# Whole float32 weights for the first unit of an attention and MoE kernel, split into two parts after that use

## The chip, the cores and the metric

The kernel runs on one core of a Trainium2 chip. The time is that of one execution on the device, in microseconds (us). The core has five engines with a queue of their own each: TensorE (PE in the profile; its weight loads are PEld), VectorE (DVE), ScalarE (ACT), GpSimd (POOL) and SyncE (SP), which issues the transfers here. An instruction waits at the head of its engine's queue until what it needs is there, so the order in which each queue is filled is part of the kernel.

## The reference

Attention over 4 batches, 8 heads, 768 positions and a head size of 64. Each position sees a window of 15 positions to either side and one summary key and value for each block of 32 positions (the maximum of the keys, the mean of the values). The result goes, as 3072 rows of 512, through two matrix products with a pointwise function between them:

```python
scores_l = scale * np.matmul(q, k.transpose(0, 1, 3, 2))          # window only
scores_s = scale * np.einsum('bhsd,bhnd->bhsn', q, k_sum) + np.log(block)
a = softmax(concatenate([scores_l_m, scores_s]))
x = matmul(a, concatenate([v, v_sum]))       # (3072, 512) after a transpose
h = x @ w_in                                 # w_in is (512, 2048)
g = h - np.tanh(h)
return (g @ w_out).astype(np.float32)        # w_out is (2048, 512)
```

The two weights are given as 64-bit floats, the result is float32.

## The kernel before

**Units.** The rows are cut into 8 units (NU) of 384 (U), two to a batch. The MoE of a unit runs over 16 blocks f of the hidden dimension (NF). For each, `moe_in` (L884) makes a 128x384 block of h in PSUM from four chunks of x, `moe_act_small` (L896) and what follows it make g from it, and `moe_out` (L944) adds g times a 128x512 block of w_out to three result tiles of 128x512, y. After f = 15 `store_y` copies the tiles out of PSUM and stores them. Attention of the later units runs beside it: in the loop over slots at the end (L1017), the MoE lags by 22 slots (LAG), 16 of which make a unit.

**Precision.** A product of two float32 operands that are held as they are is called whole here. From two operands split into a high and a low part of type float32r, a product is made as high by high, low by high and high by low, three instructions to a whole product's one call. In the kernel before, `moe_in` is split for every unit; `moe_out` is whole for unit 0 and f in WHOLE_F = {0 ... 6}, and split otherwise. `x_split` (L873) makes the two parts of x out of PSUM, `moe_split` (L938) those of g.

**Weights.** `convert(i)` (L468) brings block i of 32 (even: w_in, odd: w_out) in: a transfer of 512 KB of 64-bit words into one of three buffers (`wraw`), then the bit work that makes float32 of it in a buffer `tmp` (two) or `qa` (one): "w scale" on ScalarE or VectorE, "w shift" and "w low" on VectorE, the sign on VectorE ("w sign"), or on ScalarE and GpSimd ("w sign 1", "w sign 2") for the blocks in SIGNED. Then "w high part" (ScalarE or VectorE) and "w low part" (GpSimd or VectorE) write the two halves of the tile `w`. For the seven whole blocks the sign step writes the float32 tile `wf` instead, and `split_whole` (L528), called right after unit 0's `moe_out` of the block, makes `wh` from it, the difference in `tmp`, and a copy of that ("w low part 3") into the memory of `wf`.

**Order.** Nothing is issued in the order of the code. `do` and `either` record a task with its engines and their prices; `Plan.schedule` (L155) simulates the engines at build time, takes for each the ready task with the longest path behind it, and so fixes one order for all queues. A task with several engines gets its first one unless that is busy by more than a slack. Nudges to the path lengths and slacks are held in tables by the kind and count of a task (BIAS, KB, SL) and by thirds of the run (HALF, by count). `ring` gives a tile the memory of an earlier one of the same tag, and has it wait for all tasks that touched that one. Until 100 us (WARM) idle time of TensorE is filled with small products (`keep_warm`).

The program stands twice in the kernel; the second stands under a condition on the largest sum of squares (L283) and isn't run with these inputs.

Of the kernel before, what the change touches and what calls it, by code (L numbers as in the profile page):

```python
# [28 lines left out]

WHOLE_F = {0, 1, 2, 3, 4, 5, 6}  # L30

# [40 lines left out]
class Task:  # L72
    __slots__ = ("index", "costs", "go", "after", "order", "level", "count", "ready", "next", "start", "engine", "cost", "place", "out", "banks", "behind", "moves", "kind", "name")


# [22 lines left out]
class Plan:  # L98
# [56 lines left out]
    def schedule(self, idle):  # L155
# [16 lines left out]
        free = dict.fromkeys(engines, 0.65)  # L172
        dma = 0.0
        clock = Clock()
# [30 lines left out]
        while total:  # L205
# [20 lines left out]
            if e == PE and idle is not None:  # L226
                cost, go = idle
                if now > free[PE]:
                    free[PE] = max(free[PE], min(now, getattr(tasks[0], "out", now) + self.SEEN[POOL]))
                while free[PE] < WARM and now - free[PE] > 2 * cost + 0.1:  # L230
                    d = Task()
                    d.after, d.order, d.behind = tasks[:1], (), ()
                    d.start, d.engine, d.go = free[PE], PE, go
                    d.out = free[PE] = clock.run(free[PE], cost)
                    done.append(d)
                now = max(now, free[PE])
            t.start, t.engine, t.cost = now, e, t.costs[e]
            t.behind = [at - self.SEEN[a] for b in t.banks for a, at in used.get(b, {}).items() if a != e]
# [49 lines left out]
def program(  # L288
# [101 lines left out]
    def dma(kind, go, nbytes, run, r=(), w=()):  # L390
        do(kind, SP, nbytes / 360e3 * (2 if run < 512 else 1), go, r, w)


    fixed(("ident",), [P, P])
    fixed(("mask",), [P, SC])
    fixed(("blk",), [P, 3, NBH])
# [10 lines left out]
    def make_mask():  # L407
        gpsimd.memset(mask, 0.0)

        for lo, hi, off in ((0, 64, 0), (64 + NB, SC, 64)):  # L410
            m = mask[:, lo:hi]
            gpsimd.affine_select(m, m, [[1, hi - lo]], ALU.is_ge, BIG, base=off, channel_multiplier=-1)
            gpsimd.affine_select(m, m, [[-1, hi - lo]], ALU.is_ge, BIG, base=2 * WIN - off, channel_multiplier=1)
        gpsimd.memset(mask[:, 64:64 + NB], -LOG32)

# [13 lines left out]

    for f in range(NF):  # L430
        fixed(("w", 2 * f), [P, 2, DM], F32R)
        if f in WHOLE_F:

            buf(("wf", f), f"wf{f}", [P, DM])
            fixed(("wh", f), [P, DM], F32R)
        else:
            fixed(("w", 2 * f + 1), [P, 2, DM], F32R)

    for j in range(2):
        buf(("qf", j), f"q{j}", [P, U])  # L440
        buf(("kf", j), f"k{j}", [P, 2, KC])
    fixed(("rawq",), [P, NT, HG, D])
    fixed(("rawk",), [P, 4, HG, D])
# [24 lines left out]
    def convert(i):  # L468
# [4 lines left out]
        def load():  # L473
# [3 lines left out]
            else:  # L477
                sync.dma_start(at(raw), w_out[f * P:(f + 1) * P, :].bitcast(U32))
        dma("w load", load, P * 8 * DM, 1024, w=[(raw, 0), (raw, 1)])
        buf(tmp, "tmp", [P, DM], F32, 2) if i % 3 else buf(tmp, "qa", [P, DM], F32, 1)  # L480
# [17 lines left out]

        whole = i % 2 == 1 and f in WHOLE_F
        to = (("wf", f), 0) if whole else (tmp, 0)  # L500

# [37 lines left out]
    def top_bases(b, g):  # L539
# [3 lines left out]
        return ("th", b, g), ("tl", b, g)  # L543

    def mean_base(b, g):
        return buf(("mean", b, g), f"mean{g}", [P, HG * D], F32, 1)

# [65 lines left out]
    def place_v(b, g, tag):  # L613

        ps, x, mean = bank(("mv", b, g), tag), ("sum", b, g), mean_base(b, g)
# [5 lines left out]
        do("mean out", ACT, 0.28, lambda: scalar.activation(at(mean)[:NB], at(ps)[:NB, :HG * D], AF.Copy), r=[(ps, 0)], w=[(mean, 0)])  # L621
# [43 lines left out]
    def finish_v(b, g):  # L665
        acc, ps, mean = ("acc", 1, b, g), bank(("mv", b, g), "pT"), mean_base(b, g)
# [5 lines left out]
        do("mean out", ACT, 0.28, lambda: scalar.activation(at(mean)[:NB], at(ps)[:NB, :HG * D], AF.Copy, scale=1.0 / 32), r=[(ps, 0)], w=[(mean, 0)])  # L672

# [42 lines left out]
    def put_mean(u, g):  # L716

        mean = ("mean", u // 2, g)
        for half in range(2):
            r = 64 * (1 - half)  # L720
            dma("mean put", lambda r=r, half=half: sync.dma_start(vw[r:r + NB, :, half].rearrange("r i h d -> r i (h d)"), at(mean)[:NB].unsqueeze(1).broadcast_to([NB, NT, HG * D])),
                NT * NB * HG * D * 4, 1024, r=[(mean, 0)], w=[vw_keys(i, half)[2] for i in range(NT)])

# [82 lines left out]
    def softmax(u, p, i):  # L806
# [3 lines left out]
        def first(a):  # L810
# [6 lines left out]
            for half in range(2):  # L817
                rows, cs = slice(64 * half, 64 * half + 64), slice(64 * half, 64 * half + N2)
                vector.tensor_tensor_reduce(at(pr)[rows, a], o[rows, cs], mask[rows, cs], 1.0, 3e38, ALU.add, ALU.min, at(st)[rows, a:a + 1])

# [63 lines left out]
    def moe_in(u, f):  # L884
        xh, xl, w, ph = ("xh", u), ("xl", u), ("w", 2 * f), bank(("ph", u, f), "pH")

        def go():
            w4 = at(w).rearrange("p a (c n) -> p a c n", c=NC)
            o = at(ph)[:, :U]
            for c in range(NC):  # L890
                tensor.matmul(o, w4[:, 0, c], at(xh)[:, c], start=c == 0, stop=False)
                tensor.matmul(o, w4[:, 1, c], at(xh)[:, c], start=False, stop=False)
                tensor.matmul(o, w4[:, 0, c], at(xl)[:, c], start=False, stop=c == NC - 1)
        do("in", PE, 1.956, go, r=[(w, 0), (w, 1)] + [(x, c) for x in (xh, xl) for c in range(NC)], w=[(ph, 0)])

# [48 lines left out]
    def moe_out(u, f):  # L944
        g, w = g_base(u, f), ("w", 2 * f + 1)
        whole = u == 0 and f in WHOLE_F
        if whole:
            keys = [(g, 0), (("wf", f), 0)]
        elif f in WHOLE_F:
            keys = [(("gh", u, f), 0), (("gl", u, f), 0), (("wh", f), 0), (("wl", f), 0)]  # L950
        else:
            keys = [(("gh", u, f), 0), (("gl", u, f), 0), (w, 0), (w, 1)]
        for i in range(NT):
# [4 lines left out]
            def go(i=i, y=y):  # L958
                s = slice(P * i, P * (i + 1))
                if whole:  # L960
                    tensor.matmul(at(y), at(g)[:, s], at(("wf", f)), start=f == 0, stop=f == NF - 1)
                    return
                gh, gl = at(("gh", u, f))[:, s], at(("gl", u, f))[:, s]
                high, low = (at(("wh", f)), at(("wl", f))) if f in WHOLE_F else (at(w)[:, 0], at(w)[:, 1])
# [175 lines left out]
```

## Time and profile before

| | |
|---|---|
| time, median of three runs | 792.17 us (789.04 to 793.16) |
| the profiled execution | 788.95 us |
| its span, first to last instruction | 787.2 us |
| mean granted TensorE clock | 0.973 of full speed |
| TensorE busy, share of the span | 92% |
| VectorE busy | 67% |
| ScalarE busy | 55% |
| GpSimd busy | 37% |
| moved by DMA | 61.05 MB, mean 78 GB/s |

The profile is of one execution. A row of a group gives the line, the engine, the operation, the tile written and the tiles read, the shape, how often it ran, then the busy time in us and the mean duration in ns, then the idle time of the engine just before these instructions and what ended it. All instructions carry line 69, a helper that issues them in the planned order, so groups are told apart by their tiles: `pH` is the PSUM tile of moe_in, `pY` that of moe_out, `pS`, `pT` and `pX` those of attention. Where the memory of one tile is taken by another, a row can show an older name: the low part of a whole weight shows as `wf`. A view by stretches gives, for each stretch of the span, the time that each engine was busy (and its instructions), the granted clock, and what the DMA engines did.

### The profile page before, as it was taken

Reading aid. Unit: us, or ns where it says so; the run is one execution under the profiler, and the core shown is the slowest. Engines: PE = TensorE matmul, PEld = TensorE weight load, DVE = VectorE, ACT = ScalarE, POOL = GpSimd, SP = SyncE. Lnnn points to the kernel's source line nnn. Section 1 sums busy time; section 2 is a strip of 40 time slices with the busy share of each in tenths; the row PEclk is TensorE's granted clock in tenths of the full one; section 3 lists DMA queues with packets and bytes.
Section 4 is the critical chain, followed back from the end, with each engine's and each line's share of the span. In section 5 each row is a group of like instructions: output and inputs, shape, how many; then the busy total and the mean of one; then the engine's idle time right before and its main releaser. Section 6 shows DMA issues by size and latency. Waiting matters only on the chain.

```text
span 787.2 us, 13950 instructions
## 1 busy us (share of the span) xinstructions
PE 725.2 (92%) x4464; PEld 615.8 (78%) x4464; DVE 527.7 (67%) x1776; ACT 437.0 (56%) x1286; POOL 290.0 (37%) x390
## 2 busy tenths in 40 slices
PE   8888887777989999989899999999999999999995
PEld 6567554666878888868788888888888898889994
DVE  4878999999766767496676667476567657662221
ACT  3557765456546656546465557556665556654232
POOL 3023556666533233546323323522333232432221
PEclk9869999989999999999999999999999999999998
DMA  9876484433411121050411121031303021101001
GB/s 231 235 195 176 136 203 141 132 103 91 128 32 37 42 77 44 20 138 26 134 42 38 42 78 42 20 69 47 74 1 79 1 79 42 38 2 41 1 0 46
DMA packets 121523, 61.05 MB, mean 78 GB/s; under 512 B 92512, under 2 KB 113248, under 8 KB 121440
## 3 DMA queue, kind: packets, MB, share of 16 engines
q1 hardware_dynamic: 121440, 60.06, 28.2%
q8 instruction: 38, 0.62, 0.3%
q14 instruction: 45, 0.37, 0.2%
HBM read 51.38 MB, written 6.29 MB: 73 GB/s over the span
## 4 chain that ended last, share of the span: by engine, by line
PE 65%; DVE 23%; DMA 3%; issue 3%; ACT 2%; POOL 2%; SPq 0%; POOLq 0%; DVEq 0%; ACTq 0%
PE pH L69 27%; PE pY L69 26%; DVE prob L69 6%; PE pS L69 6%; DVE tmp L69 4%; PE pT L69 4%; DVE qa L69 3%; DVE top L69 2%; PE pX L69 2%; DVE k L69 2%; DVE stat L69 1%; POOL wraw L69 1%; DVE gl L69 1%; DMA wraw<-in_moe_w_out_dram 1%; DVE w L69 1%
## 5 line engine op out<-in xcount | busy, mean ns | idle before, releaser
L69 PE MATMUL pH<-xh,w 128*128 128x384 f32 x1024 | 273.5, 347 | 15.3 <-POOL w L69 7.9
L69 POOL TENSOR_TENSOR gv<-gu,gt 128x384 f32<-128x384 f32 x116 | 118.3, 1020 | 315.4 <-ACT gu L69 184.2
L69 PEld LDWEIGHTS pH<-xh,w 128*128 128x128 f32 x1024 | 187.9, 192 | 29.3 <-POOL w L69 11.2
L69 PE MATMUL pH<-xl,w 128*128 128x384 f32 x512 | 175.3, 342 | 1.0 <-DVE xl L69 1.0
L69 ACT ACTIVATE gu<-pH 128x384 f32<-128x384 f32 x128 | 62.5, 488 | 172.5 <-PE pH L69 164.2
L69 PE MATMUL pY<-w,gh 128*128 128x512 f32 x432 | 140.7, 407 | 0.0
L69 DVE CUSTOM_DVE_ANT_0 prob<-pS,mask 64x118 f32<-64x118 f32 x352 | 97.9, 278 | 42.6 <-PE pT L69 28.5
L69 ACT ACTIVATE prob<-prob,stat 128x118 f32<-128x118 f32 x195 | 76.4, 393 | 58.1 <-DVE stat L69 52.2
L69 PEld LDWEIGHTS pH<-xl,w 128*128 128x128 f32 x512 | 98.3, 192 | 1.7 <-DVE xl L69 1.7
L69 DVE CAST gh<-gv 128x384 fp32r<-128x384 f32 x74 | 30.4, 410 | 85.7 <-POOL gv L69 79.2
L69 PE MATMUL pY<-w,gl 128*128 128x512 f32 x216 | 85.1, 394 | 0.7 <-DVE gl L69 0.7
L69 PEld LDWEIGHTS pY<-w,gh 128*128 128x128 f32 x432 | 75.0, 190 | 10.9 <-issue 0.5
L69 PE MATMUL pY<-wf,gh 128*128 128x512 f32 x189 | 79.2, 442 | 0.0
L69 ACT ACTIVATE gu<-gu 128x384 f32<-128x384 f32 x128 | 66.7, 522 | 0.0
L69 PE MATMUL pS<-k,q 128*128 128x364 f32 (+1 forms) x176 | 48.9, 357 | 14.7 <-DVE stat L69 12.1
L69 ACT ACTIVATE gt<-pH 128x384 f32<-128x384 f32 x128 | 61.7, 482 | 0.1
L69 PE MATMUL pY<-wh,gh 128*128 128x512 f32 x147 | 61.5, 418 | 0.0
L69 DVE TENSOR_TENSOR gl<-gv,gh 128x384 fp32r<-128x384 f32 x90 | 54.1, 601 | 7.4 <-ACT gh L69 2.3
L69 PE MATMUL pY<-wh,gl 128*128 128x512 f32 x147 | 58.4, 397 | 0.0
L69 DVE TENSOR_SCALAR prob<-prob,stat 128x118 f32<-128x118 f32 x184 | 55.3, 337 | 2.3
L69 PEld LDWEIGHTS pS<-k,q 128*128 128x128 f32 x176 | 29.4, 192 | 30.4 <-issue 18.8
L69 DVE TENSOR_SCALAR stat<-stat 128x2 f32<-128x2 f32 x95 | 27.9, 294 | 31.3 <-ACT prob L69 31.0
(161 smaller groups left out, 1164.3 us busy)
## 6 DMA issues: line engine op xcount, KB each, us to landing
wraw<-in_moe_w_in_dram SPq DMA_DIRECT2D x16, 512.0 KB
wraw<-in_moe_w_out_dram SPq DMA_DIRECT2D x16, 512.0 KB
rawq<-in_q_dram SPq DMA_DIRECT2D x48, 128.0 KB
out_dram<-tmp SPq DMA_DIRECT2D x24, 256.0 KB
rawk<-in_k_dram SPq DMA_DIRECT2D x32, 128.0 KB
vw<-in_v_dram SPq DMA_DIRECT2D x40, 96.0 KB
vw<-in_v_dram SPq DMA_DIRECT2D x48, 64.0 KB
wraw<-in_k_dram SPq DMA_DIRECT2D x16, 192.0 KB
```

Source lines behind the costliest of these rows:

```text
L69: return lambda *args, **kwargs: self._tc.keep_in_program_order(op(*args, **kwargs))
```

## The change

All 32 weight blocks are whole for unit 0, and so is x of unit 0: `x_split` makes one float32 copy in the memory of the high part, `moe_in` of unit 0 multiplies whole, `moe_out` of unit 0 is whole for all f, and g of unit 0 is not split. `split_whole` is called after each of these uses. It writes the high part to a tile of its own and the low part straight into the float32 tile of the block before it in the order of use (into a tile `wl` for the first), which "w low part 3" is dropped for. The units from 1 on use the two parts as before.

```diff
-WHOLE_F = {0, 1, 2, 3, 4, 5, 6}
+WHOLE_IN = True
+WHOLE_F = set(range(16))
...
+    wholes = sorted((i for i in range(2 * NF) if (WHOLE_IN if i % 2 == 0 else i // 2 in WHOLE_F)), key=lambda i: i // 2 + 1.5 * (i % 2))
+    for i in range(2 * NF):
+        if i in wholes:
+            buf(("wf", i), f"wf{wholes.index(i)}", [P, DM])
+            fixed(("wh", i), [P, DM], F32R)
         else:
-            fixed(("w", 2 * f + 1), [P, 2, DM], F32R)
+            fixed(("w", i), [P, 2, DM], F32R)
...
-        whole = i % 2 == 1 and f in WHOLE_F
-        to = (("wf", f), 0) if whole else (tmp, 0)
+        whole = i in wholes
+        to = (("wf", i), 0) if whole else (tmp, 0)
...
-    def split_whole(f):
+    def split_whole(i):
 
-        x, high, tmp, low = ("wf", f), ("wh", f), buf(("wd", f), "tmp", [P, DM], F32, 2), buf(("wl", f), f"wf{f}", [P, DM], F32R)
+        n = wholes.index(i)
+        x, high, low = ("wf", i), ("wh", i), buf(("wl", i), f"wf{n - 1}" if n else "wl", [P, DM], F32R)
         either("w high part 2", {ACT: 0.52, DVE: 0.335}, lambda e: copy(e, at(high), at(x)), r=[(x, 0)], w=[(high, 0)])
-        either("w low part 2", {POOL: 1.225, DVE: 0.602}, lambda e: e.tensor_tensor(at(tmp), at(x), at(high).bitcast(F32), op=ALU.subtract), r=[(x, 0), (high, 0)], w=[(tmp, 0)])
-        either("w low part 3", {ACT: 0.52, DVE: 0.335}, lambda e: copy(e, at(low), at(tmp)), r=[(tmp, 0)], w=[(low, 0)])
+        either("w low part 2", {POOL: 1.225, DVE: 0.602}, lambda e: e.tensor_tensor(at(low), at(x), at(high).bitcast(F32), op=ALU.subtract), r=[(x, 0), (high, 0)], w=[(low, 0)])
...
     def x_split(u, p):
         px = px_base(u, p)
+        if u == 0 and WHOLE_IN:
+            xf = buf(("xf", u), "xh", [P, NC, U], F32, 2) if p == 0 else ("xf", u)
+            either("x whole", {ACT: 0.371, DVE: 0.465}, lambda e: copy(e, at(xf)[:, p], at(px)[:, :U]), r=[(px, i) for i in range(NT)], w=[(xf, p)])
+            return
...
+        if u == 0 and i in wholes:
+            def go():
+                for c in range(NC):
+                    tensor.matmul(at(ph)[:, :U], at(("wf", i))[:, P * c:P * (c + 1)], at(xf)[:, c], start=c == 0, stop=c == NC - 1)
+            do("in", PE, 2.65, go, r=[(("wf", i), 0)] + [(xf, c) for c in range(NC)], w=[(ph, 0)])
+            split_whole(i)
+            return
...
-        do("in", PE, 1.956, go, r=[(w, 0), (w, 1)] + [(x, c) for x in (xh, xl) for c in range(NC)], w=[(ph, 0)])
+        do("in", PE, 2.1, go, r=w_keys(i) + [(x, c) for x in (xh, xl) for c in range(NC)], w=[(ph, 0)])
...
-            do("out", PE, 0.856 if whole else 0.648, go, r=keys, w=[(y, 0)])
+            do("out", PE, 0.866 if whole else 0.695, go, r=keys, w=[(y, 0)])
         if whole:
-            split_whole(f)
+            split_whole(w)
```

The planner changes in three places: the prices of "in" and "out" above, the price of a transfer by the length of its runs, and a rule that a VectorE task of some kinds, if it would start while a GpSimd task of over 0.3 us runs, is taken to start at that one's end:

```diff
-        do(kind, SP, nbytes / 360e3 * (2 if run < 512 else 1), go, r, w)
+        rate = 227e3 if run < 512 else 302e3 if run < 1024 else 356e3 if run < 4096 else 390e3
+        do(kind, SP, nbytes / rate, go, r, w)
...
+HELD = {"w shift", "w low", "w sign", "w low part", "w low part 2", "w low part 3", "w high part", "w high part 2", "w scale", "normal", "g high", "g low", "g", "cube", "big", "k again", "q again", "top pre", "sum guard"}
...
+            if e == DVE and t.kind in HELD and now >= held[0]:
+                now = max(now, held[1])
+            if e == POOL and t.costs[e] > 0.3:
+                held = now, now + t.costs[e]
```

Three tiles become smaller or shared: the mask keeps the 118 columns that a half of the partitions reads (L817 to L819, the same instructions on `mask[rows]`), built by more GpSimd instructions at the start; the block means of both groups of heads lie in one tile, at 32 partitions a group; and the key maxima of both groups of heads, for batches 2 and 3, use the memory `top0` one after the other.

```diff
-    fixed(("mask",), [P, SC])
+    fixed(("mask",), [P, N2])
...
+    fixed(("mean",), [P, HG * D])
+    mean, MEAN = made[("mean",)], [(("mean",), g) for g in range(NG)]
...
-        acc = buf(("acc", which, b, g), "vacc" if which else f"top{g}", [P, D] if which else [P, 2, D])
+        acc = buf(("acc", which, b, g), "vacc" if which else "top0", [P, D] if which else [P, 2, D])
```

More of the change, by code (lines that the diff above doesn't have):

```diff
@@ L172, in schedule @@
         free = dict.fromkeys(engines, 0.65)
-        dma = 0.0
+        dma, held = 0.0, (0.0, 0.0)
         clock = Clock()
@@ L408, in make_mask @@
         gpsimd.memset(mask, 0.0)
-        for lo, hi, off in ((0, 64, 0), (64 + NB, SC, 64)):
-            m = mask[:, lo:hi]
+        for half, lo, hi, off in ((0, 0, 64, 0), (0, 64 + NB, N2, 64), (1, NB, N2, 0)):
+            m = mask[64 * half:64 * half + 64, lo:hi]
             gpsimd.affine_select(m, m, [[1, hi - lo]], ALU.is_ge, BIG, base=off, channel_multiplier=-1)
             gpsimd.affine_select(m, m, [[-1, hi - lo]], ALU.is_ge, BIG, base=2 * WIN - off, channel_multiplier=1)
-        gpsimd.memset(mask[:, 64:64 + NB], -LOG32)
+        for half in range(2):
+            gpsimd.memset(mask[64 * half:64 * half + 64, 64 * (1 - half):64 * (1 - half) + NB], -LOG32)
     def make_blk():
@@ L427, in program @@
     do("const", DVE, 0.05, lambda: vector.memset(small, -GC), w=[SMALL])
[L430 to L435, printed above, removed]
+    wholes = sorted((i for i in range(2 * NF) if (WHOLE_IN if i % 2 == 0 else i // 2 in WHOLE_F)), key=lambda i: i // 2 + 1.5 * (i % 2))
[3 more added lines that the diff above has]
+            fixed(("wh", i), [P, DM], F32R)
         else:
-            fixed(("w", 2 * f + 1), [P, 2, DM], F32R)
+            fixed(("w", i), [P, 2, DM], F32R)
     for j in range(2):
@@ L478, in load @@
                 sync.dma_start(at(raw), w_out[f * P:(f + 1) * P, :].bitcast(U32))
-        dma("w load", load, P * 8 * DM, 1024, w=[(raw, 0), (raw, 1)])
+        dma("w load", load, P * 8 * DM, 1024 if i % 2 == 0 else 4096, w=[(raw, 0), (raw, 1)])
         buf(tmp, "tmp", [P, DM], F32, 2) if i % 3 else buf(tmp, "qa", [P, DM], F32, 1)
@@ L526, in convert, with w_keys, w_parts @@
             either("w low part", {POOL: 1.225, DVE: 0.602}, lambda e: e.tensor_tensor(at(res)[:, 1], at(tmp), at(res)[:, 0].bitcast(F32), op=ALU.subtract), r=[(tmp, 0), (res, 0)], w=[(res, 1)])
-    def split_whole(f):
-        x, high, tmp, low = ("wf", f), ("wh", f), buf(("wd", f), "tmp", [P, DM], F32, 2), buf(("wl", f), f"wf{f}", [P, DM], F32R)
+    def split_whole(i):
+        n = wholes.index(i)
+        x, high, low = ("wf", i), ("wh", i), buf(("wl", i), f"wf{n - 1}" if n else "wl", [P, DM], F32R)
         either("w high part 2", {ACT: 0.52, DVE: 0.335}, lambda e: copy(e, at(high), at(x)), r=[(x, 0)], w=[(high, 0)])
-        either("w low part 2", {POOL: 1.225, DVE: 0.602}, lambda e: e.tensor_tensor(at(tmp), at(x), at(high).bitcast(F32), op=ALU.subtract), r=[(x, 0), (high, 0)], w=[(tmp, 0)])
-        either("w low part 3", {ACT: 0.52, DVE: 0.335}, lambda e: copy(e, at(low), at(tmp)), r=[(tmp, 0)], w=[(low, 0)])
+        either("w low part 2", {POOL: 1.225, DVE: 0.602}, lambda e: e.tensor_tensor(at(low), at(x), at(high).bitcast(F32), op=ALU.subtract), r=[(x, 0), (high, 0)], w=[(low, 0)])
+    def w_keys(i):
+        return [(("wh", i), 0), (("wl", i), 0)] if i in wholes else [(("w", i), 0), (("w", i), 1)]
+    def w_parts(i):
+        return (at(("wh", i)), at(("wl", i))) if i in wholes else (at(("w", i))[:, 0], at(("w", i))[:, 1])
     top_of = {}
@@ L543, in top_bases @@
         return ("th", b, g), ("tl", b, g)
-    def mean_base(b, g):
-        return buf(("mean", b, g), f"mean{g}", [P, HG * D], F32, 1)
     def load_part(kind, b, p, h, tag):
@@ L613, in place_v @@
     def place_v(b, g, tag):
-        ps, x, mean = bank(("mv", b, g), tag), ("sum", b, g), mean_base(b, g)
+        ps, x = bank(("mv", b, g), tag), ("sum", b, g)
         def go():
@@ L620, in place_v @@
         do("mean turn", PE, 0.5, go, r=[(x, pr) for pr in range(PG)] + [IDENT], w=[(ps, 0)])
-        do("mean out", ACT, 0.28, lambda: scalar.activation(at(mean)[:NB], at(ps)[:NB, :HG * D], AF.Copy), r=[(ps, 0)], w=[(mean, 0)])
+        do("mean out", ACT, 0.28, lambda: scalar.activation(mean[32 * g:32 * g + NB], at(ps)[:NB, :HG * D], AF.Copy), r=[(ps, 0)], w=[MEAN[g]])
     def sum_chunks(b, g, which):
-        acc = buf(("acc", which, b, g), "vacc" if which else f"top{g}", [P, D] if which else [P, 2, D])
+        acc = buf(("acc", which, b, g), "vacc" if which else "top0", [P, D] if which else [P, 2, D])
         for c in range(4):
@@ L665, in finish_v @@
     def finish_v(b, g):
-        acc, ps, mean = ("acc", 1, b, g), bank(("mv", b, g), "pT"), mean_base(b, g)
+        acc, ps = ("acc", 1, b, g), bank(("mv", b, g), "pT")
         def go():
@@ L671, in finish_v @@
         do("mean turn", PE, 0.44, go, r=[(acc, 0), IDENT], w=[(ps, 0)])
-        do("mean out", ACT, 0.28, lambda: scalar.activation(at(mean)[:NB], at(ps)[:NB, :HG * D], AF.Copy, scale=1.0 / 32), r=[(ps, 0)], w=[(mean, 0)])
+        do("mean out", ACT, 0.28, lambda: scalar.activation(mean[32 * g:32 * g + NB], at(ps)[:NB, :HG * D], AF.Copy, scale=1.0 / 32), r=[(ps, 0)], w=[MEAN[g]])
     def load_qk(u, g):
@@ L716, in put_mean @@
     def put_mean(u, g):
-        mean = ("mean", u // 2, g)
         for half in range(2):
             r = 64 * (1 - half)
-            dma("mean put", lambda r=r, half=half: sync.dma_start(vw[r:r + NB, :, half].rearrange("r i h d -> r i (h d)"), at(mean)[:NB].unsqueeze(1).broadcast_to([NB, NT, HG * D])),
-                NT * NB * HG * D * 4, 1024, r=[(mean, 0)], w=[vw_keys(i, half)[2] for i in range(NT)])
+            dma("mean put", lambda r=r, half=half: sync.dma_start(vw[r:r + NB, :, half].rearrange("r i h d -> r i (h d)"), mean[32 * g:32 * g + NB].unsqueeze(1).broadcast_to([NB, NT, HG * D])),
+                NT * NB * HG * D * 4, 1024, r=[MEAN[g]], w=[vw_keys(i, half)[2] for i in range(NT)])
     def operands(u, p):
@@ L818, in first @@
                 rows, cs = slice(64 * half, 64 * half + 64), slice(64 * half, 64 * half + N2)
-                vector.tensor_tensor_reduce(at(pr)[rows, a], o[rows, cs], mask[rows, cs], 1.0, 3e38, ALU.add, ALU.min, at(st)[rows, a:a + 1])
+                vector.tensor_tensor_reduce(at(pr)[rows, a], o[rows, cs], mask[rows], 1.0, 3e38, ALU.add, ALU.min, at(st)[rows, a:a + 1])
         def exps(a):
@@ L884, in moe_in @@
     def moe_in(u, f):
-        xh, xl, w, ph = ("xh", u), ("xl", u), ("w", 2 * f), bank(("ph", u, f), "pH")
+        xh, xl, xf, i, ph = ("xh", u), ("xl", u), ("xf", u), 2 * f, bank(("ph", u, f), "pH")
+        if u == 0 and i in wholes:
[5 more added lines that the diff above has]
+            return
         def go():
-            w4 = at(w).rearrange("p a (c n) -> p a c n", c=NC)
+            high, low = (x.rearrange("p (c n) -> p c n", c=NC) for x in w_parts(i))
             o = at(ph)[:, :U]
             for c in range(NC):
-                tensor.matmul(o, w4[:, 0, c], at(xh)[:, c], start=c == 0, stop=False)
-                tensor.matmul(o, w4[:, 1, c], at(xh)[:, c], start=False, stop=False)
-                tensor.matmul(o, w4[:, 0, c], at(xl)[:, c], start=False, stop=c == NC - 1)
-        do("in", PE, 1.956, go, r=[(w, 0), (w, 1)] + [(x, c) for x in (xh, xl) for c in range(NC)], w=[(ph, 0)])
+                tensor.matmul(o, high[:, c], at(xh)[:, c], start=c == 0, stop=False)
+                tensor.matmul(o, low[:, c], at(xh)[:, c], start=False, stop=False)
+                tensor.matmul(o, high[:, c], at(xl)[:, c], start=False, stop=c == NC - 1)
+        do("in", PE, 2.1, go, r=w_keys(i) + [(x, c) for x in (xh, xl) for c in range(NC)], w=[(ph, 0)])
     def moe_act_small(u, f):
@@ L944, in moe_out @@
     def moe_out(u, f):
-        g, w = g_base(u, f), ("w", 2 * f + 1)
+        g, w = g_base(u, f), 2 * f + 1
         whole = u == 0 and f in WHOLE_F
[L947 to L952, printed above, removed]
+        keys = [(g, 0), (("wf", w), 0)] if whole else [(("gh", u, f), 0), (("gl", u, f), 0), *w_keys(w)]
         for i in range(NT):
@@ L960, in go @@
                 if whole:
-                    tensor.matmul(at(y), at(g)[:, s], at(("wf", f)), start=f == 0, stop=f == NF - 1)
+                    tensor.matmul(at(y), at(g)[:, s], at(("wf", w)), start=f == 0, stop=f == NF - 1)
                     return
                 gh, gl = at(("gh", u, f))[:, s], at(("gl", u, f))[:, s]
-                high, low = (at(("wh", f)), at(("wl", f))) if f in WHOLE_F else (at(w)[:, 0], at(w)[:, 1])
+                high, low = w_parts(w)
                 tensor.matmul(at(y), gh, high, start=f == 0, stop=False)
```

## The prediction

> **What bounds the kernel now.** I read the page first, then busy time by stretches cut at the events of the first unit, then the waits of TensorE inside the stretch that differs, then the groups of VectorE there, and last the timeline and the chain where one operation had to be priced.
>
> ```profile
> span 787.2 us, 13950 instructions
> ...
> PE 725.2 (92%) x4464; PEld 615.8 (78%) x4464; DVE 527.7 (67%) x1776; ACT 437.0 (56%) x1286; POOL 290.0 (37%) x390
> ```
>
> The averages say TensorE. Cut at the events of the first unit they say otherwise:
>
> ```profile
> core 0: us, PE busy (x) PEld busy (x) DVE busy (x) ACT busy (x) POOL busy (x), PEclk, DMA share, GB/s
> 0.00:63.00 63.00, 53.07 (x481) 40.15 (x481) 43.58 (x216) 32.66 (x102) 12.40 (x34) 0.86 0.84 218
> 63.00:201.00 138.00, 109.67 (x538) 81.79 (x539) 128.69 (x291) 85.55 (x224) 83.71 (x77) 0.94 0.46 136
> 201.00:225.00 24.00, 21.27 (x104) 18.28 (x103) 19.04 (x49) 11.66 (x32) 9.71 (x15) 0.93 0.43 125
> 225.00:787.20 562.20, 541.22 (x3345) 475.57 (x3343) 336.41 (x1223) 307.08 (x929) 184.14 (x265) 1.00 0.18 45
> ```
>
> The view of a tile gives the cuts (median and extreme durations in ns, first and last start in us):
>
> ```profile
> L69 PE MATMUL pH<-xh,w x1024: 333/336/739, 63.6 to 771.9; 128*128 128x384 f32 x171
> ```
>
> ```profile
> L69 ACT ACTIVATE tmp<-pY x24: 577/598/612, 200.9 to 780.9; 128x512 f32<-128x512 f32 x24
> ```
>
> Between 63.6 us (first moe_in product) and 200.9 us (first result of unit 0 copied out of PSUM) lies the MoE of unit 0: 137 us with VectorE 93% busy (128.69 of 138). From 225 us on TensorE is 96% busy (541.22 of 562.20): the other seven units are bound by it and take some 83 us each ((780.9 - 200.9)/7). Inside the first stretch TensorE waits for weights:
>
> ```profile
> PE pH L69 <- POOL w L69: 7.9, 6, 1.9
> ```
>
> ```profile
> PEld pH L69 <- POOL w L69: 11.2, 9, 2.3
> ```
>
> "POOL w" is the low part, the last link of a weight's conversion (scale, shift, low bits, sign, high part, low part). So unit 0 is paced by the conversion of 32 blocks, whose fullest engine is VectorE, and by the two links at its end, which the change takes off the path.
>
> **The change part by part.**
>
> *TensorE in unit 0.* Every moe_in of unit 0 becomes 4 whole float32 products for 12 split ones, and nine moe_out become 3 whole for 9 split (seven are whole already). Two stretches of the timeline, then two pieces of the chain:
>
> ```profile
> 123.98 1.88 PE L69 MATMUL pY<-wf,gh 128*128 128x512 f32 x4
> ...
> 130.78 2.74 PE L69 MATMUL pY<-wf,gh 128*128 128x512 f32 x6
> ```
>
> ```profile
> 712.09 6.25 PE pH L69 x36
> 718.34 2.08 PE pY L69 x9
> ```
>
> One whole product stands in the trace as two instructions. Three whole tiles against two: 2.74 - 1.88 = 0.86 us for 512 columns; a split tile takes 2.08/3 = 0.69, a split moe_in 6.25/3 = 2.08. No whole product of 384 columns with a weight is in the trace; I scale 0.86 by 384/512 to 0.65, 2.6 us a block (the ends are 2.08, as if it cost no more than the split one, and 4 x 0.86 = 3.4). That adds 16 x 0.5 + 9 x 3 x 0.17 = 8 + 4.6 = 12.6 us of TensorE work. Unit 0's MoE then needs 16 x (2.6 + 2.6) = 83 us. Attention lies beside it:
>
> ```profile
> L69 PE MATMUL pH<-xl,w 128*128 128x384 f32 x76 | 28.4, 374 | 0.9 <-DVE xl L69 0.9
> ...
> L69 PE MATMUL pS<-k,q 128*128 128x364 f32 x23 | 10.0, 509 | 4.0 <-DVE stat L69 4.0
> ```
>
> The 76 products of the first row are 19 blocks of moe_in (4 each): unit 0's 16 and three of unit 1. Of the 109.67 us busy, MoE takes 19 x 2.08 + 21 whole tiles x 0.86 + some 26 split ones x 0.69 = 76, so attention has at most 34, and at least the 10.0 of its largest group; since pipelined durations count too much I take 18. So TensorE can't end unit 0 before 63.6 + 83 + 18 = 165 us (157 to 181), against 201 now: the 12.6 us lie in its present waits, with some 36 us of room. Were that cover gone, they would be a loss of 12.6.
>
> *VectorE in unit 0.* These groups of the stretch are touched:
>
> ```profile
> L69 DVE SCALAR_TENSOR_TENSOR tmp<-wraw,tmp 128x512 uint32<-128x512 uint32 x28 | 25.7, 919 | 0.4
> L69 DVE SCALAR_TENSOR_TENSOR qa<-wraw,qa 128x512 uint32<-128x512 uint32 x16 | 17.1, 1068 | 0.2
> ...
> L69 DVE TENSOR_TENSOR gl<-gv,gh 128x384 fp32r<-128x384 f32 x8 | 5.6, 699 | 0.2
> ...
> L69 DVE CAST gh<-gv 128x384 fp32r<-128x384 f32 x5 | 4.7, 941 | 1.2 <-POOL wraw L69 1.2
> ...
> L69 DVE CAST w<-qa 128x512 fp32r<-128x512 f32 x4 | 3.4, 858 | 1.1 <-POOL qa L69 1.0
> L69 DVE CAST w<-tmp 128x512 fp32r<-128x512 f32 x8 | 3.4, 420 | 0.0
> ...
> L69 DVE TENSOR_TENSOR tmp<-wf,wh 128x512 f32<-128x512 f32 x4 | 2.7, 678 | 0.0
> L69 DVE CAST wh<-wf 128x512 fp32r<-128x512 f32 x3 | 2.3, 763 | 2.4 <-POOL wf L69 2.4
> ```
>
> The first two are the bit work of the conversion; they stay. The split of g goes for f 7 to 15: about 7 of the 8 gl and 4 of the 5 gh, 4.9 + 3.8 = 8.7. The high parts (3.4 + 3.4 + 2.3 = 9.1) and the low parts of the whole weights (2.7) no longer stand ahead of unit 0's product; until unit 1 they may run on ScalarE, first choice for a high part and 62% busy here (85.55 of 138), on GpSimd, or behind. One x low goes too (about 0.5, like a gl). The sum is 21. The ends are 9 (high and low parts stay on VectorE inside the stretch) and 27 (the waits of 2.4, 1.2 and 1.1 go as well, and a further microsecond of x low before 63). I take 21, since ScalarE has 52 us free and 15 more casts at the 0.6 us of its copy of that shape are 9. So 128.7 - 21 = 108 us of VectorE, 116 at the present density of 93%. Off each block also goes the latency of the last two links; TensorE's waits for it price that at up to 7.9 + 11.2 = 19, at least 0 where VectorE is late anyway. VectorE is nearly full, so I take 3. Unit 0 ends at 63.6 + 116 - 3 = 177.
>
> *GpSimd's share.* The low parts stay 32 in number; seven ScalarE copies (low part 3, 0.6 each, beside other work) go. A stretch 24 us shorter with almost the same GpSimd work has it 83.7/114 = 73% busy instead of 61%. That matters because VectorE stands still under some GpSimd instructions:
>
> ```profile
> 146.27 3.67 POOL L69 TENSOR_TENSOR w<-tmp,w 128x512 fp32r<-128x512 f32 x2 [1.23 <-DVE w L69]
> ```
>
> ```profile
> 147.17 3.33 DVE L69 SCALAR_TENSOR_TENSOR qa<-wraw,qa 128x512 uint32<-128x512 uint32 x2
> ```
>
> ```profile
> L69 DVE SCALAR_TENSOR_TENSOR tmp<-wraw,tmp x30: 669/692/1950, 42.6 to 180.7; 128x512 uint32<-128x512 uint32 x30
> ```
>
> Two operations of 0.69 (median) take 3.33 beside two GpSimd subtractions. Over the two conversion groups that is 28 x (919 - 692) + 16 x (1068 - 692) ns = 12.4 us of standing still. At 73/61 of it, 2.5 more; I take 2 (0 to 5). So unit 0 ends at **179 us**.
>
> The Trainium skill, "SBUF — State Buffer", section "Who interferes with whom", states the cause as a lock: a VectorE instruction with two SBUF inputs, or in a two-port mode, blocks for the whole of a GpSimd instruction that holds the shared pair. The 3.33 us above agrees. It speaks against this change, which postpones GpSimd's reads and removes few; followed to its end it gives the second rival below.
>
> *The new wait.* A low part is written into the float32 tile of the weight before it in order of use, so it waits for that weight's products and splits. Behind it in GpSimd's fixed order stand the products g and the signs, and TensorE's moe_out waits for g. The price lies between 0 and the present waits for "POOL w" (19.1 us); I take 0, since that wait replaces another of the same engine, and one low part falls due per 2.6 us of TensorE work.
>
> *After unit 0.* Of what is done by 201 us now, three moe_in of unit 1 (6.3 us) would still be to do. The rest is 787.2 - 201 + 6.3 = 592.5. The late splits lie beside TensorE's work: VectorE is 60% and GpSimd 33% busy from 225 us on. Even 32 low parts of 1.8 us (3.67/2) wholly after unit 0, 59 us, fit into the 83 of unit 1.
>
> *Costed at nothing.* The mask is built narrower but read by the same instructions; its few more GpSimd instructions fall before 63 us, where GpSimd is busy for 12.4. Means and the key maximum get other memory, used one after the other as now. The planner's new prices issue nothing; they reorder, which is the third rival.
>
> **Sum.** 179 + 592.5 = 771.5 us of span; the profiled execution took 788.95 for a span of 787.2, so 1.75 lie around it: 773.2. That execution is below all three timed runs (789.04 to 793.16, median 792.17), so I state a little more, **774**.
>
> **Rivals.**
> 1. *TensorE becomes the bound of unit 0.* VectorE gives way more than I count (27 us, and its waits). Unit 0 ends at 165; time 165 + 592.5 + 1.75 = 759. For it: VectorE's lead over TensorE is only 128.69 to 109.67. Against: a fixed order with two engines near 90% seldom has no waits.
> 2. *The work is moved, not removed.* Each low part runs as soon as it may, inside the stretch; VectorE saves 9, loses 5 to standing still, and TensorE's 12.6 more is partly uncovered (0 to all). Time 789 - 4 to 789 + 8, around 790. For it: the 3.33 row. Against: the largest wait of pH is for "POOL w", and goes.
> 3. *The later order gets worse.* All instructions stand in one order planned at build time, with nudges bound to names and counts of tasks; "w high part" vanishes, and unit 1's first "x high" is number 0 where it was 4. The place is 225 us onward:
>
> ```profile
> 300.00:350.00 50.00, 47.78 (x298) 41.13 (x296) 35.52 (x117) 26.59 (x82) 23.90 (x36) 1.00 0.28 71
> 350.00:375.00 25.00, 22.18 (x159) 18.57 (x159) 17.42 (x57) 14.02 (x41) 13.17 (x24) 1.00 0.15 51
> ```
>
> In 350 to 375 TensorE is 88.7% busy, over all from 225 us 96.3%. If half of these 562 us came to look like that stretch, they would take 281 x (96.3/88.7 - 1) = 24 us more: 773 + 24 = 797, slower than before. It decides once the idle time there, 21 us now, doubles. Against: TensorE leads there, and VectorE has 40% free.
>
> **How the numbers follow.** My forecast (762 to 784) 0.53; rival 1 0.15; rival 2 0.16; rival 3 0.16. About 0.5% (4 us) is what a measurement of this kernel tells from no change. Faster by more takes the forecast, rival 1 and an edge of rival 2: 0.71. Within it lies most of rival 2: 0.13. Slower 0.16. The range reaches from near the floor of rival 1 to the middle of rival 3: 757 to 797.
>
> **What would show it.** Right: the first result of unit 0 copied out near 179 instead of 201 us; TensorE at 90% or more between 63 and that point; no waits of pH for "POOL w" before unit 1; a whole moe_in near 2.6 us. If VectorE is under 85% there, rival 1 held; if it is still at 93% over the same 138 us, rival 2; if unit 0 ends early and the time does not follow, idle TensorE time after it shows rival 3. A whole moe_in of 3.4 us would cost 13 us of the room, not of the forecast. What would break it altogether: a moe_out of unit 0 late because its g stands behind a waiting low part.

## The result, and the profile after

The changed kernel takes 769.55 us (median of four runs, 766.32 to 770.96) against 791.73 us before (789.04 to 793.16): 0.972 of the time, with an interval of 0.968 to 0.976. 774 was predicted. The profiled execution has a span of 764.5 us against 787.2. Of all executions told of below one stands apart: one of four of the changed kernel with the old planner took 1783 us where the others agree within 0.5 us, and its figures leave that one out.

The page of the changed kernel, its span and the busy time of each engine (share of the span, instructions):

```profile
span 764.5 us, 13760 instructions
...
PE 719.3 (94%) x4373; PEld 593.0 (78%) x4373; DVE 499.0 (65%) x1702; ACT 453.5 (59%) x1318; POOL 299.0 (39%) x406
```

The view by stretches of the changed kernel, with the cuts that the prediction used (columns as there):

```profile
0.00:63.00 63.00, 53.45 (x497) 41.26 (x498) 45.08 (x217) 34.58 (x108) 13.38 (x39) 0.92 0.82 214
63.00:201.00 138.00, 119.68 (x521) 69.56 (x519) 123.12 (x286) 98.29 (x257) 99.36 (x97) 1.00 0.51 154
201.00:225.00 24.00, 23.35 (x149) 20.75 (x146) 14.81 (x59) 13.49 (x42) 9.90 (x16) 1.00 0.08 17
225.00:764.50 539.50, 522.86 (x3215) 461.41 (x3213) 315.99 (x1145) 307.17 (x913) 176.39 (x256) 0.99 0.19 48
```

Between 63 and 201 us TensorE works 10 us more than before, ScalarE 13 and GpSimd 16 more, and VectorE 6 less. Two views of tiles of the changed kernel give the cuts of unit 0, and the timeline the price of a whole moe_in:

```profile
L70 PE MATMUL pH<-xh,wf x548: 332/338/590, 59.9 to 749.8; 128*128 128x384 f32 x183
```

```profile
L70 ACT ACTIVATE tmp<-pY x24: 575/597/609, 190.8 to 758.3; 128x512 f32<-128x512 f32 x24
```

```profile
59.89 2.75 PE L70 MATMUL pH<-xh,wf 128*128 128x384 f32 x8
62.47 0.78 PE L70 MATMUL pS<-k,q 128*128 128x364 f32 x2
```

Unit 0 begins at 59.9 us (63.6 before), and its first result is copied out at 190.8 (200.9). The next instruction follows a whole moe_in after 62.47 - 59.89 = 2.58 us; 2.6 was the estimate. By 190.8 us TensorE has done four moe_in of unit 1, against three before. Without them, at 2.09 each, unit 0 ends at 182.4 instead of 194.6: 12 us of the 22.7 between the two spans. The other 10 come after unit 0, where the prediction had none. Over the run, scores wait less for the softmax of earlier tiles; the same group of the page, before and then after:

```profile
L69 PE MATMUL pS<-k,q 128*128 128x364 f32 (+1 forms) x176 | 48.9, 357 | 14.7 <-DVE stat L69 12.1
```

```profile
L70 PE MATMUL pS<-k,q 128*128 128x364 f32 (+1 forms) x176 | 45.8, 341 | 6.0 <-DVE stat L70 5.9
```

The whole weights leave the work of scores alone. This is a first sign that something else was at work, the order.

### The profile page after: what moved, and what is told of

It is laid out like the page before. It is cut to its first block, busy times and chain, and to the rows that moved or that the text cites. A ratio compares the mean times of both kernels' runs of the same rounds, so it can differ in the third digit from the quotient of the medians.

```text
span 764.5 us, 13760 instructions
## 1 busy us (share of the span) xinstructions
PE 719.3 (94%) x4373; PEld 593.0 (78%) x4373; DVE 499.0 (65%) x1702; ACT 453.5 (59%) x1318; POOL 299.0 (39%) x406
## 5 line engine op out<-in xcount | busy, mean ns | idle before, releaser
L70 PE MATMUL pH<-xh,wf 128*128 128x384 f32 x548 | 186.0, 373 | 7.0 <-DVE wf L70 3.4
L70 PE MATMUL pY<-wf,gh 128*128 128x512 f32 x432 | 177.9, 439 | 0.0
L70 PE MATMUL pH<-xh,wh 128*128 128x384 f32 x448 | 154.0, 344 | 0.0
L70 PE MATMUL pH<-xl,wh 128*128 128x384 f32 x448 | 151.2, 337 | 0.0
L70 PE MATMUL pY<-wh,gh 128*128 128x512 f32 x336 | 140.8, 419 | 0.9 <-ACT tmp L70 0.9
L70 PE MATMUL pY<-wh,gl 128*128 128x512 f32 x336 | 132.1, 393 | 0.0
L70 PEld LDWEIGHTS pH<-xh,wf 128*128 128x128 f32 x548 | 102.2, 188 | 29.6 <-POOL wf L70 6.5
L70 PEld LDWEIGHTS pY<-wf,gh 128*128 128x128 f32 x432 | 80.6, 189 | 21.7 <-issue 11.5
L70 PEld LDWEIGHTS pH<-xh,wh 128*128 128x128 f32 x448 | 84.3, 188 | 3.5 <-issue 0.5
L70 PEld LDWEIGHTS pH<-xl,wh 128*128 128x128 f32 x448 | 84.1, 188 | 0.0
```

What stands on the lines that cost most here:

```text
L70: return lambda *args, **kwargs: self._tc.keep_in_program_order(op(*args, **kwargs))
```

## The experiments

Theory A, that of the prediction: the whole weights bring the gain, by taking work and two links off the conversion of unit 0. Rival B: the planner's changes bring it, by another order. Times are medians; ratios are to the kernel before, run on the same chip, with intervals.

**The planner's changes alone.** The kernel before, with the new prices and the rule for VectorE beside GpSimd; the weights as they were.

```diff
+            if e == DVE and t.kind in HELD and now >= held[0]:
+                now = max(now, held[1])
+            if e == POOL and t.costs[e] > 0.3:
+                held = now, now + t.costs[e]
...
-        do(kind, SP, nbytes / 360e3 * (2 if run < 512 else 1), go, r, w)
+        rate = 227e3 if run < 512 else 302e3 if run < 1024 else 356e3 if run < 4096 else 390e3
+        do(kind, SP, nbytes / rate, go, r, w)
...
-        do("in", PE, 1.956, go, r=[(w, 0), (w, 1)] + [(x, c) for x in (xh, xl) for c in range(NC)], w=[(ph, 0)])
+        do("in", PE, 2.1, go, r=[(w, 0), (w, 1)] + [(x, c) for x in (xh, xl) for c in range(NC)], w=[(ph, 0)])
...
-            do("out", PE, 0.856 if whole else 0.648, go, r=keys, w=[(y, 0)])
+            do("out", PE, 0.866 if whole else 0.695, go, r=keys, w=[(y, 0)])
```

> The kernel before with nothing but the planner's new prices and its rule for VectorE beside GpSimd; no weight is whole that was not. Theory A (the gain comes from the whole weights, which take two links off the conversion of unit 0): 785 to 797 us, within 6 us of before. Rival B (the gain, or the 10 us of it that fell after unit 0, comes from a better order): 770 to 782 us, and the results of units 1 to 3 come out earlier by 5 us or more against unit 0's.

769.91 us (768.97 to 772.93), ratio 0.972 (0.968 to 0.976). That is the whole gain of the change, with none of its weights. In its profile the first results of units 0 to 3 are copied out at 191.9, 269.7, 358.1 and 442.7 us, against 200.9, 283.5, 372.2 and 458.7 before. Units 1 to 3 thus come 5 to 7 us less behind unit 0, as rival B expected. Theory A falls for the kernel as it stands.

**The whole weights alone.** The changed kernel with the old planner.

```diff
-            if e == DVE and t.kind in HELD and now >= held[0]:
-                now = max(now, held[1])
...
-        rate = 227e3 if run < 512 else 302e3 if run < 1024 else 356e3 if run < 4096 else 390e3
-        do(kind, SP, nbytes / rate, go, r, w)
+        do(kind, SP, nbytes / 360e3 * (2 if run < 512 else 1), go, r, w)
...
-        do("in", PE, 2.1, go, r=w_keys(i) + [(x, c) for x in (xh, xl) for c in range(NC)], w=[(ph, 0)])
+        do("in", PE, 1.956, go, r=w_keys(i) + [(x, c) for x in (xh, xl) for c in range(NC)], w=[(ph, 0)])
```

> The changed kernel with the old planner: old prices of transfers, moe_in and moe_out, no rule for VectorE beside GpSimd (a whole moe_in still priced 2.65). Theory A: 766 to 776 us, most of the 22 us stays. Rival B: 778 to 790 us.

782.79 us (median of three), ratio 0.989 (0.984 to 0.995): 9 us of gain, inside rival B's range. The view by stretches of this kernel, up to its first result of unit 0 at 198.2 us:

```profile
60.00:198.00 138.00, 117.65 (x453) 64.74 (x452) 114.27 (x291) 88.67 (x233) 82.55 (x81) 0.94 0.49 146
```

VectorE is relieved, 83% busy (114.27 of 138) where it was 93%, and the unit takes as long as before. Two of TensorE's waits from 63 to 190 us show what it waits for instead:

```profile
PE pH L70 <- ACT gt L70: 7.0, 4, 4.3
PE pT L70 <- DVE prob L70: 5.6, 3, 3.8
```

moe_in waits here for the tanh of an earlier block to free its bank, and a transpose for the softmax. Neither is a weight. That these instructions come too early in the fixed order is a reading of the waits; no run tests it.

**The changed kernel without the rule.** New prices, but no rule.

```diff
-            if e == DVE and t.kind in HELD and now >= held[0]:
-                now = max(now, held[1])
-            if e == POOL and t.costs[e] > 0.3:
-                held = now, now + t.costs[e]
```

> The changed kernel without the planner's rule for VectorE beside GpSimd, all else as changed. Theory A: 766 to 775 us. Rival B, if the rule is what makes the order better: 775 us or more, with more VectorE time in the stretch of unit 0.

793.07 us, ratio 1.001 (0.998 to 1.003). Without the rule the changed kernel has no gain at all. Its TensorE waits for "ACT gt" too, 8.4 us in the same stretch. The other half of rival B's expectation, more VectorE time, did not come. Up to its first result of unit 0, at 202.7 us, VectorE works 116.7 us, where the changed kernel has 120.2 (60 to 191 us, shown further down), and few of the splits of w and g are left on VectorE from 0 to 230 us:

```profile
60.00:203.00 143.00, 119.42 (x444) 65.80 (x444) 116.70 (x287) 87.49 (x229) 82.21 (x84) 0.92 0.48 142
```

```profile
L70 DVE TENSOR_TENSOR wf<-wf,wh 128x512 fp32r<-128x512 f32 x7 | 6.1, 874 | 4.2 <-POOL wf L70 4.1
L70 DVE CAST gh<-gv 128x384 fp32r<-128x384 f32 x5 | 2.2, 443 | 3.6 <-PE pY L70 3.6
L70 DVE TENSOR_TENSOR gl<-gv,gh 128x384 fp32r<-128x384 f32 x4 | 2.2, 552 | 0.2
...
L70 DVE CAST wh<-wf 128x512 fp32r<-128x512 f32 x2 | 0.8, 414 | 0.0
```

These are 11 splits (parts of g and high parts of w) and 7 low parts of w; in the changed kernel they are 8 and 2. Less work on VectorE is not enough for a gain.

**The rule alone, and the prices alone.** The kernel before with one of the two. The rule, the prices of before kept:

```diff
+            if e == DVE and t.kind in HELD and now >= held[0]:
+                now = max(now, held[1])
+            if e == POOL and t.costs[e] > 0.3:
+                held = now, now + t.costs[e]
```

and the prices, without these four lines:

```diff
-        do(kind, SP, nbytes / 360e3 * (2 if run < 512 else 1), go, r, w)
+        rate = 227e3 if run < 512 else 302e3 if run < 1024 else 356e3 if run < 4096 else 390e3
+        do(kind, SP, nbytes / rate, go, r, w)
...
-            do("out", PE, 0.856 if whole else 0.648, go, r=keys, w=[(y, 0)])
+            do("out", PE, 0.866 if whole else 0.695, go, r=keys, w=[(y, 0)])
```

> The kernel before, its old prices, with nothing new but the planner's rule for VectorE beside GpSimd. Theory C (the rule makes the planned order keep to what VectorE can do, and brings the gain by itself): 767 to 776 us. Rival D (the order is a draw, and rule and prices together happened on a good one): anywhere from 772 to 800, as likely above 780 as below. Theory A, in what is left of it (the rule gives nothing without the whole weights): 785 to 797.

> The kernel before with the planner's new prices of transfers, moe_in and moe_out, without the rule. Theory C: no gain or a loss, 786 to 803 us, as the same prices without the rule cost the changed kernel 10 us against the old ones. Rival D: anywhere from 772 to 800. If prices alone bring it: 766 to 776.

The rule alone: 767.75 us (764.16 to 770.34), ratio 0.967 (0.962 to 0.973). The prices alone: 790.83, ratio 0.997 (0.994 to 0.999). So it is the rule. With the prices alone TensorE's largest wait from 63 to 190 us is again the one for "ACT gt", 11.2 us, though the weights are as before. The rule issues nothing; it changes the times that the planner reckons with, and by them who gets a task, and in what order. Groups of VectorE from 0 to 230 us in the kernel before:

```profile
L69 DVE TENSOR_TENSOR gl<-gv,gh 128x384 fp32r<-128x384 f32 x12 | 9.0, 751 | 0.4
L69 DVE CAST gh<-gv 128x384 fp32r<-128x384 f32 x9 | 6.6, 732 | 3.7 <-PE pY L69 2.4 <-POOL wraw L69 1.2
```

and, as the prediction showed, 12 casts of w and 3 of wh. The same view of the kernel with the rule alone, where no cast of wh is left on VectorE:

```profile
L69 DVE CAST gh<-gv 128x384 fp32r<-128x384 f32 x5 | 5.2, 1063 | 2.5 <-POOL gv L69 2.5
L69 DVE TENSOR_TENSOR gl<-gv,gh 128x384 fp32r<-128x384 f32 x3 | 2.1, 714 | 0.1
...
L69 DVE CAST w<-tmp 128x512 fp32r<-128x512 f32 x1 | 1.7, 1728 | 1.2 <-POOL tmp L69 1.2
L69 DVE CAST w<-qa 128x512 fp32r<-128x512 f32 x1 | 1.4, 1401 | 0.0
```

36 of these tasks stood on VectorE (12, 9, 12 and 3); 10 do with the rule. They are of the kinds that the prediction took off VectorE by means of the whole weights. The old planner prices VectorE without the time in which it stands still, finds it free too early, and gives it work that ScalarE and GpSimd could take. The stretch up to unit 0's first result, at 187.2 us, with the rule alone:

```profile
63.60:187.00 123.40, 105.93 (x539) 78.67 (x539) 107.58 (x246) 94.70 (x246) 92.41 (x80) 0.96 0.50 146
```

VectorE works 107.6 us up to that result where it was 128.1 from 63.6 to 201; ScalarE and GpSimd have some 9 us more each, in 14 us less. That these moves are what brings the time fits the rows, but isn't shown: the rule changes the order too, no run parts the two, and the changed kernel without the rule has few such tasks on VectorE and no gain.

**w_in alone.** WHOLE_F is {0 ... 6} again, the 16 blocks of w_in stay whole.

```diff
-WHOLE_F = set(range(16))
+WHOLE_F = {0, 1, 2, 3, 4, 5, 6}
```

> The changed kernel with the 16 blocks of w_in whole, and of w_out only the seven that were whole before. Theory A says that both halves count by the blocks freed: 16 of the 25 newly whole blocks are here, so 0.64 of 22 us, about 778 us (773 to 783). If only moe_in's wait for its low part counted (it was the wait with the largest sum), 768 to 772.

770.93 us, ratio 0.974 (0.970 to 0.978). By the second reading of the expectation this looked like moe_in's wait for its low part. Beside the planner's changes alone, 769.91, it says nothing of the kind: any of these weights comes out at 770 under the new planner.

**Is TensorE the bound of unit 0 now?** moe_in of unit 0 with two of its four chunks, in the same planned order.

```diff
-                for c in range(NC):
+                for c in range(0, NC, 2):
-                    tensor.matmul(at(ph)[:, :U], at(("wf", i))[:, P * c:P * (c + 1)], at(xf)[:, c], start=c == 0, stop=c == NC - 1)
+                    tensor.matmul(at(ph)[:, :U], at(("wf", i))[:, P * c:P * (c + 1)], at(xf)[:, c], start=c == 0, stop=c == NC - 2)
```

> The changed kernel in the same planned order, but moe_in of unit 0 multiplies only chunks 0 and 2 of the four: half of the sum over the inner dimension is left out, 16 x 1.3 = 21 us of TensorE work. If TensorE bounds unit 0 now: 749 to 756 us. If the conversion of the weights still paces it (theory A): unit 0's result at most 5 us earlier, 764 to 770 us.

768.85 us (766.39 to 770.89), the changed kernel's time. 21 us of TensorE work in unit 0 were covered, as the prediction had the added 12.6 covered. The time lies in theory A's range; unit 0's result, expected up to 5 us earlier, came 4 us later in the profiled execution (last section).

**What do the low parts cost on GpSimd?** Their 32 tasks keep their place in the plan and issue nothing; units 1 to 7 read the high part in their stead.

```diff
-        either("w low part 2", {POOL: 1.225, DVE: 0.602}, lambda e: e.tensor_tensor(at(low), at(x), at(high).bitcast(F32), op=ALU.subtract), r=[(x, 0), (high, 0)], w=[(low, 0)])
+        either("w low part 2", {POOL: 1.225, DVE: 0.602}, lambda e: None, r=[(x, 0), (high, 0)], w=[(low, 0)])
...
-        return (at(("wh", i)), at(("wl", i))) if i in wholes else (at(("w", i))[:, 0], at(("w", i))[:, 1])
+        return (at(("wh", i)), at(("wh", i))) if i in wholes else (at(("w", i))[:, 0], at(("w", i))[:, 1])
```

> The changed kernel in the same planned order with the 32 low parts of the weights left out; units 1 to 7 multiply by the high part twice. It takes some 40 us of GpSimd work out of the stretch of unit 0. If VectorE's standing still beside GpSimd is what holds unit 0 back: VectorE's bit operations of the conversion at their medians, unit 0's result 6 to 12 us earlier, 757 to 764 us. If not: 766 to 771 us.

The time, 1570 us, can't be used: h is doubled from unit 1 on, its sum of squares passes the limit of L283, and the second program runs as well. The first program's part of the trace can be read (the view of a tile counts both programs):

```profile
L70 ACT ACTIVATE tmp<-pY x48: 576/598/607, 180.2 to 1563.5; 128x512 f32<-128x512 f32 x48
```

Unit 0's first result comes at 180.2 us, 10.6 earlier than in the changed kernel and inside the 6 to 12 expected. Bit operations of the conversion from 63 to 191 us, in the changed kernel and then without low parts:

```profile
L70 DVE SCALAR_TENSOR_TENSOR tmp<-wraw,tmp 128x512 uint32<-128x512 uint32 x19 | 17.2, 909 | 0.2
L70 DVE TENSOR_SCALAR tmp<-tmp 128x512 uint32<-128x512 uint32 x18 | 14.0, 783 | 1.7 <-ACT tmp L70 1.6
L70 DVE SCALAR_TENSOR_TENSOR wf<-wraw,tmp 128x512 uint32<-128x512 uint32 x10 | 12.3, 1230 | 0.0
```

```profile
L70 DVE SCALAR_TENSOR_TENSOR tmp<-wraw,tmp 128x512 uint32<-128x512 uint32 x19 | 13.0, 688 | 0.2
L70 DVE TENSOR_SCALAR tmp<-tmp 128x512 uint32<-128x512 uint32 x18 | 9.8, 547 | 7.9 <-ACT tmp L70 7.7
L70 DVE SCALAR_TENSOR_TENSOR wf<-wraw,tmp 128x512 uint32<-128x512 uint32 x10 | 8.7, 868 | 0.0
```

The first group falls to 688 ns, its median before (692); the other two fall too, but not to their medians of 0.42 and 0.69 us. These three groups alone give back 12 us of VectorE. So the low parts on GpSimd hold unit 0 back by some 10 us now. That this goes through VectorE fits the 12 us. GpSimd's own signs and products g also lose a queue ahead of them, and this run doesn't tell the two apart.

**Do the tables of nudges matter?** BIAS, KB and SL emptied, in four kernels.

```diff
...
+BIAS = {}
...
+SL = {}
...
+KB = {}
```

> The kernel before with the three tables of nudges emptied. Together with the next run it tells whether the gain hangs on how the tables happen to fit. If they matter much: 800 to 840 us; if little: 790 to 800.

> The changed kernel with the three tables of nudges emptied. Theory A: 15 to 30 us below the kernel before without nudges, since the links off the path do not depend on the order. If the gain were an accident of the order: no steady difference, within 8 us of it.

> The kernel before with the whole new planner and empty tables of nudges; it differs from the changed kernel with empty tables (778.7 us) only in the weights of unit 0 and the memory. Theory C says that whole weights add nothing under the new planner: 775 to 783 us. Theory A: 785 us or more.

> The changed kernel with the old planner and empty tables of nudges; it differs from the kernel before with empty tables (779.8 us) only in the weights of unit 0 and the memory. If whole weights gain 9 us under the old planner whatever the nudges, as they did with them: 768 to 774 us. If that 9 was a draw of the order: 775 to 790. Theory C, for the rule: over 778.7 us, which is this kernel with the rule and the new prices.

779.80 us for the kernel before, 778.68 for the changed one, 775.07 for the old weights with the new planner, 782.56 for the whole weights with the old one. The first lies below both ranges expected of it, the second within 8 us of the first, as an accident of the order would. All of the grid, medians in us (those of the kernel before lie between 791.73 and 793.13 on the chips of these runs, so a difference of 1 or 2 us says nothing):

| tables | planner | weights as before | all whole in unit 0 | whole minus before |
|---|---|---|---|---|
| full | old | 791.7 | 782.8 | -9 |
| full | new prices | 790.8 | 793.1 | +2 |
| full | rule | 767.8 | not run | |
| full | both | 769.9 | 769.6 | 0 |
| empty | old | 779.8 | 782.6 | +3 |
| empty | both | 775.1 | 778.7 | +4 |

In the last column nothing is steady: under one planner the whole weights are worth between -9 and +4 us, and about nothing in the kernel as it is. The rule is worth 21 to 25 us with the full tables (prices held alike) and, together with the prices, 4 to 5 with empty ones. The tables can give VectorE work that has another engine: some slacks in SL are negative, -0.6 for "g high", "g low" and "w high part". The kernel before with empty tables leaves one of the 36 tasks on VectorE, a cast of w from tmp:

```profile
L69 DVE CAST w<-tmp 128x512 fp32r<-128x512 f32 x1 | 0.4, 423 | 0.0
```

which fits the little that the rule is worth there. The order is another one altogether: unit 0 runs from 120.1 us (first moe_in) to 223.5 (first result), later than in the kernel before, and the time is 12 us shorter all the same. With the new planner the tables save 5 and 9 us, with the old one they cost 12 and 0: they fit a planner that has the rule.

## Why the prediction was right, and where its reasons failed

**The number held, the cause did not.** 774 was predicted and 769.55 came. But the planner's rule alone gives 767.8, and whole weights beside the new planner add nothing. That the sum came within 5 us is luck: the whole weights were to give 18 us and give nothing beside the rule, and the rule, counted at nothing, gives 25. The step that failed is the one under "Costed at nothing": "The planner's new prices issue nothing; they reorder, which is the third rival." The third rival had the cause, another order, but the wrong sign, and only part of the place: with the rule alone the span is 20.9 us shorter (766.3 against 787.2), and 13.7 of them are there at unit 0's first result (187.2 against 200.9).

**The signs that the prediction named** came in part. The first result of unit 0 is copied out at 190.8 us, not near 179; less unit 1's four moe_in that is 182.4, after a start 3.7 us earlier than before. TensorE is 87% busy up to there (113.54 of 131 us, shown below), not 90, and waits for weights still:

```profile
PE pH L70 <- DVE wf L70: 3.4, 2, 2.5
PE pH L70 <- POOL wf L70: 2.8, 3, 1.4
```

VectorE is 92% busy (120.22 of 131), near the 93 that was to show the second rival. A moe_out late for its g, which would have broken the forecast, isn't among the waits.

**The bound of the stretch** was read rightly as far as it is not TensorE: half of moe_in taken away changes nothing, while the low parts taken off GpSimd shorten VectorE's operations and bring unit 0's first result 10.6 us forward. VectorE's busy time alone doesn't set the end: the whole weights with the old planner take 14 us off it (114.27 against 128.1), and the result comes 2.7 us earlier (198.2 against 200.9).

**The price of whole products** was right (2.58 against 2.6 us), and so was its cover.

**The relief of VectorE, 21 us,** was counted rightly by tasks: where 36 splits stood on VectorE up to 230 us, the changed kernel has 8 (3 gl, 3 gh, 2 wh). In time VectorE kept most of it, 120.2 us busy from 60 to 191 against 128.1 from 63.6 to 201:

```profile
60.00:191.00 131.00, 113.54 (x468) 63.90 (x467) 120.22 (x271) 94.22 (x247) 92.59 (x86) 1.00 0.49 149
```

**Why that relief bought nothing** is told by the two runs of one half each. With the new planner it had been had already: the rule alone moves 26 of the 36 tasks. With the old one VectorE was relieved, but TensorE then waited for "ACT gt" and "DVE prob".

**Standing still beside GpSimd** was sized at 2 us more; it is 12. Over the conversion's bit operations up to 230 us, busy time less count by median (50 of 0.69, 32 of 0.42 us) is 17.7 us before and 29.5 after. GpSimd's share came as forecast, 71% (92.59 of 131 us) against 73; the step that scales the standing still with that share failed. The rise goes with the planner more than with the weights: the figure is 27.2 us with the rule alone, 21.3 with the rule and the prices, and only 11.4 with the whole weights and the old planner; shares can't be told from that. The rule doesn't avoid the standing still. It reckons with it, gives VectorE less and GpSimd more, and VectorE then stands still more and still ends earlier. The Trainium skill ("SBUF — State Buffer", section "Who interferes with whom") states the lock that the prediction told of: one of the two engines blocks for the whole of the other's instruction. The rise agrees with it, and so does the first result of unit 0, 10.6 us earlier without the low parts. That the old planner left such standing still out is what the prediction had in its rows and didn't use.

**After unit 0** 592.5 us were predicted and 764.5 - 182.4 = 582.1 measured. No term stood for these 10 us; they more than make up for the 3 us by which unit 0 ended later than the 179 of the sum.

**The second rival,** work moved and not removed with a time near 790, comes nearest to what the whole weights do where the planner is held alike: 0 us under the new one, and +3 and +4 with empty tables (but -9 under the old one with full tables). Its condition held: of the 32 low parts 29 run on GpSimd inside the stretch of unit 0, with starts from 64.2 to 189.0 us:

```profile
L70 POOL TENSOR_TENSOR wf<-wf,wh 128x512 fp32r<-128x512 f32 x29 | 42.8, 1474 | 1.0
```

**What stays open.** By which of its two effects the rule brings the gain, other engines or another order, isn't settled. Nor is why the whole weights gain 9 us under the old planner and lose 2 with new prices; each new order may be a draw, and no run measures how large such draws are. Whole weights with the rule and the old prices were not run, nor was the new memory of mask, means and key maxima by itself.

## What to carry to other kernels

Where an order is planned at build time, a change to the planner's prices is a change to the kernel: cost it first, by looking for prices that the trace contradicts (0.6 in the plan for an operation whose mean was 0.92) and for the tasks that would go to another engine if they were right. Split a change into its order and its work and run both halves before believing either, best under two settings of the tables. And when work moves to GpSimd, charge VectorE for it: here the low parts there held unit 0 back by 10.6 us.

## What was not expected of the hardware

With half of moe_in left out, unit 0's first result came later, not earlier, in the profiled execution, at 195.1 us instead of 190.8. Its stretch shows a mean granted TensorE clock of 0.90, where the changed kernel has 1.00:

```profile
60.00:195.00 135.00, 105.21 (x408) 58.19 (x407) 118.17 (x275) 94.88 (x246) 95.02 (x88) 0.90 0.51 148
```

The TensorE with more gaps (78% busy against 87%) had the lower clock. Over the whole run it was 0.971 to 0.977 in four executions with half of moe_in, and 0.978 to 0.990 in four of the changed kernel. That the gaps cause it, and that it undid the work saved, isn't shown; the times agree (768.85 and 769.55 us).
